# Side tasks of a planned attention kernel hand TensorE single groups of 512 columns instead of pairs, and the order is remade

## The chip, the core and the metric

The kernel runs on one core of a Trainium2 chip. The metric is the device time of one execution in microseconds. All times here are medians of several runs or come from one profiled execution, and the text says which.

## What is computed

Two attention blocks read the same input and are mixed by a gate. The reference, cut to its core (S = 2048, D = 512, 32 heads of 16 columns):

```python
g = sigmoid((x * gate_w).sum(-1, keepdims=True))
# A: softmax attention
scores = einsum("bhqd,bhkd->bhqk", q, k) * (Dh ** -0.5)
a = einsum("bhqk,bhkd->bhqd", softmax(scores), v) @ A_wo
# B: linear attention, phi(t) = where(t > 0, t + 1, exp(t)) + 1e-6
kv = einsum("bhsd,bhse->bhde", phi(k), v);  z = phi(k).sum(over s)
b = (einsum("bhqd,bhde->bhqe", phi(q), kv) / (phi(q) . z + 1e-6)) @ B_wo
out = g * a + (1 - g) * b
```

Each block has its own q, k, v (x times a 512 x 1536 matrix).

## The kernel before

**Units.** The softmax block is cut into 2048 units: one head, 512 query columns, 128 keys. Four heads stand in the four row strips of TensorE (K of 16 rows padded to 32), so a score group S is up to four matmuls of 512 columns that run beside each other (`s_fn`, built by `cand_s`). Each unit's scores fill one PSUM bank of 128 x 512. There are eight banks, and one of them gathers the attention's result.

**Two ways to the exponential.** Of each S group the first two units usually lie in two banks side by side and go to ScalarE, one activation of 128 x 1024 (line 1141, `cand_exp`, tile P). The others go to VectorE, which makes an approximate power of two from the scores in int16 (tile Z), two banks at once (line 1053) or one bank (line 1089, `cand_op1`); GpSimd adds two shifted copies of it (line 1115, `cand_shift`), whose sum with weights is the exponential. TensorE then multiplies P or Z with the values: a PV group of up to four matmuls of 17 x 512 in the four column strips (`cand_pv`, tiles Vp and Vs; the 17th row is the softmax's sum).

**Side tasks.** All else is written as generators that yield one step at a time, an operation with its engine and what it reads and writes: the projections K (`t_k`), Q (`t_q`) and V (`t_v`), phi of the linear block's keys (`t_phik`), x times phi(k) (`t_mt`), the sums and the state (`t_z`, `t_kv`, `t_m`), phi of its queries (`t_phiq`), the denominators (`t_den`), the gathering of a finished round (`aout`) and the last products with both output matrices for 128 rows (`t_final`). Their matmuls stand in the four column strips (`mm4`: 4 matmuls of 32 x 512), so one product over 128 rows of the contraction is one quad, and `pe4` packs a list of quads into one step. A step is indivisible: its matmuls stand one after the other on TensorE, and the last of them alone raises TensorE's semaphore.

**The order is made by a planner in the kernel.** It runs when the program is built. Each engine has a time at which it is free, each tile a time at which it is written or read. At each turn all candidates (a score group, a PV group, an exponential, a VectorE or GpSimd operation, the next step of the first few side tasks by due time) are compared by when they could start and by a priority, and the first is issued. The knobs of these choices stand in the dictionary `DEF`, and the table `PLAN` has a row of other values for each eight units issued (257 rows, lines 181 to 439). `TS` gives release and due times of the side tasks. Where TensorE would idle for 200 ns and more, `fill` puts dummy matmuls. TensorE has two forms here: S groups in row form, all else in column form; the planner counts a change between them.

**Waits.** Each engine has one semaphore, raised by each step (`_Eng.add`, `emit`); every matmul of the kernel but those of two transposes is recorded at line 639 (`mm`), so tiles tell them apart. DMAs are issued from SyncE's queue (lines 619 to 623): the masked copies of Q (eight of 16 KB for each of 15 tiles), the way of a finished round through DRAM (`oad`, transposed into `OAT`), the denominators, the outputs.

Of the kernel before, what the change touches and what calls it, by code (L numbers as in the profile page):

```python
# [145 lines left out]
def bass_gated_mix__mha_block__linear_attn_block__prompt_kernel(  # L146
# [22 lines left out]
    def spl(t):  # L169
# [12 lines left out]
        0: {"DSL": 0.0, "PWN": 600.0, "RIDE": 600.0, "SLK": -100.0, "REL": 1.0, "TST": 610, "PRE": 150, "O1P": 440, "ACP": 450, "EAR": 300.0, "RSV": 400.0, "TMX": 2.0, "O1W": 300.0},  # L182
        1: {"SKEW": 0, "PWT": 250.0, "HP": 160.0, "SLK": -100.0, "UEX": 0.6, "REL": 0.5, "PORT": 1, "TST": 900, "SWP": -1, "TMX": 2.0},
        2: {"DSL": 0.0, "PWT": 250.0, "HP": 160.0, "HD": 200.0, "NDB": 1, "SLK": -100.0, "UEX": -0.3, "REL": 1.0, "PORT": 1, "SGL": 410, "TST": 900, "O1P": 440, "EAR": 300.0, "RSV": 400.0, "DMX": 4.0},
        3: {"PWT": 100.0, "TPR": 650, "HD": 60.0, "NDB": 1, "UEX": -0.3, "REL": 1.0, "PORT": 1, "SGL": 410, "O1P": 410, "SWP": 1, "EAR": 300.0},
        4: {"PWT": 250.0, "HD": 0.0, "NDB": 1, "SLK": 250.0, "ROOM": 2, "REL": 1.0, "PORT": 1, "TST": 900, "O1P": 440, "EAR": 300.0, "RSV": 200.0, "DMX": 4.0},
        5: {"DSL": 0.0, "DTOL": 250.0, "PWN": 100.0, "UEX": -0.3, "REL": 1.0, "PORT": 1, "SGL": 410, "TST": 900, "PRE": 0, "O1P": 440, "EAR": 300.0, "NAJ": 1.0},
        6: {"PWN": 100.0, "NDB": 1, "REL": 1.0, "PORT": 1, "SGL": 410, "PRE": 300, "O1P": 440, "EAR": 300.0, "O1W": 300.0, "DMX": 2.0, "NAJ": 1.0},
        7: {"PWE": 100.0, "HD": 60.0, "NDB": 1, "SLK": -100.0, "PORT": 1, "SGL": 410, "PRE": 150, "O1P": 440, "SWP": 1, "EAR": 300.0, "TMX": 2.0, "NAJ": 1.0},
        8: {"SKEW": 3, "DSL": 0.0, "PWT": 100.0, "PWN": 900.0, "HP": 160.0, "HD": 0.0, "NDB": 1, "SLK": -100.0, "REL": 0.5, "SGL": 410, "TST": 900, "O1P": 440, "EAR": 150.0, "TMX": 2.0, "NAJ": 1.0},  # L190
        9: {"SKEW": 6, "PWN": 900.0, "HD": 0.0, "UEX": -0.3, "SGL": 395, "TST": 610, "ACP": 450, "SWP": 1, "NAJ": 1.0},
        10: {"PWN": 900.0, "HD": 0.0, "SLK": -100.0, "SGL": 395, "TST": 900, "PRE": 150, "O1P": 410, "SWP": 1, "TMX": 2.0, "NAJ": 1.0},
        11: {"PWN": 200.0, "TPR": 450, "SLK": -100.0, "TOP": 800, "REL": 1.0, "PRE": 0, "O1P": 440, "SWP": -1, "EAR": 300.0, "TMX": 2.0},
        12: {"DSL": 40.0, "DTOL": 2000.0, "PWE": 100.0, "PWN": 200.0, "TOP": 800, "PORT": 1, "PRE": 150, "SWP": 1, "DMX": 4.0, "NAJ": 1.0},
        13: {"SKEW": 6, "DTOL": 2000.0, "PWT": 250.0, "PWN": 100.0, "TPR": 650, "SLK": -100.0, "REL": 1.0, "SGL": 410, "TST": 900, "O1P": 440, "SWP": -1, "EAR": 900.0, "TMX": 2.0, "DMX": 4.0, "NAJ": 1.0},
        14: {"SKEW": 6, "DTOL": 2000.0, "PWT": 250.0, "PWN": 100.0, "TPR": 650, "RIDE": 900.0, "SLK": -100.0, "REL": 1.0, "SGL": 410, "TST": 900, "O1P": 440, "SWP": 1, "EAR": 900.0, "TMX": 2.0, "DMX": 4.0, "NAJ": 1.0},
        15: {"SKEW": 6, "DSL": 40.0, "PWN": 900.0, "TPR": 450, "RIDE": 900.0, "HD": 60.0, "UEX": 0.6, "ROOM": 2, "REL": 1.0, "SGL": 395, "TST": 610, "ACP": 450, "SWP": 1},
        16: {"SKEW": 0, "DSL": 150.0, "PWE": 50.0, "PWT": 250.0, "PWN": 900.0, "TPR": 720, "RIDE": 1800.0, "HP": 160.0, "HD": 60.0, "UEX": 0.6, "REL": 0.5, "TST": 900, "PRE": 0, "O1P": 440, "SWP": 1, "TMX": 2.0},
        17: {"SKEW": 6, "UEX": -0.3, "REL": 1.0, "PORT": 1, "SGL": 395, "TST": 610, "ACP": 450, "SWP": 1, "NAJ": 1.0},
        18: {"SKEW": 6, "PWT": 250.0, "PWN": 100.0, "SLK": -100.0, "REL": 1.0, "SGL": 410, "TST": 900, "O1P": 440, "SWP": -1, "EAR": 900.0, "TMX": 2.0},  # L200
        19: {"PWT": 250.0, "HP": 160.0, "HD": 60.0, "SLK": -100.0, "ROOM": 2, "REL": 1.0, "PORT": 1, "SGL": 410, "TST": 900, "PRE": 0, "O1P": 440, "SWP": 1, "TMX": 2.0, "DMX": 4.0},
        20: {"DTOL": 2000.0, "PWT": 250.0, "TPR": 720, "RIDE": 600.0, "HD": 60.0, "SLK": 0.0, "REL": 1.0, "PORT": 1, "TST": 610, "PRE": 0, "O1P": 440, "SWP": 1, "TMX": 2.0, "DMX": 2.0},
        21: {"DTOL": 2000.0, "PWT": 250.0, "TPR": 720, "RIDE": 600.0, "HD": 60.0, "SLK": 0.0, "ROOM": 2, "REL": 1.0, "PORT": 1, "TST": 610, "PRE": 0, "O1P": 440, "ACP": 450, "SWP": 1, "TMX": 2.0, "DMX": 2.0},
        22: {"DTOL": 1000.0, "PWT": 250.0, "TPR": 720, "RIDE": 600.0, "HD": 60.0, "SLK": 0.0, "ROOM": 2, "REL": 1.0, "PORT": 1, "TST": 610, "PRE": 0, "O1P": 440, "ACP": 450, "TMX": 2.0, "DMX": 2.0},
        23: {"PWE": 100.0, "PWT": 250.0, "TPR": 650, "HP": 160.0, "SLK": 0.0, "ROOM": 2, "REL": 1.0, "SGL": 410, "TST": 900, "PRE": 150, "O1P": 440, "ACP": 450, "SWP": 1, "DMX": 4.0},
        24: {"SKEW": 6, "PWT": 250.0, "PWN": 100.0, "SLK": -100.0, "REL": 1.0, "SGL": 410, "TST": 900, "O1P": 440, "SWP": -1, "EAR": 900.0, "TMX": 2.0},
        25: {"SKEW": 6, "PWN": 100.0, "SLK": -100.0, "REL": 1.0, "SGL": 410, "TST": 900, "O1P": 440, "SWP": -1, "EAR": 900.0, "TMX": 2.0},
        26: {"PWT": 250.0, "HP": 160.0, "SLK": -100.0, "ROOM": 1, "REL": 1.0, "PORT": 1, "SGL": 410, "TST": 900, "PRE": 300, "O1P": 440, "SWP": 1, "TMX": 2.0, "DMX": 4.0},
        27: {"PWT": 250.0, "HP": 160.0, "ROOM": 2, "REL": 1.0, "PORT": 1, "SGL": 410, "TST": 900, "PRE": 150, "O1P": 440, "ACP": 450, "SWP": 1, "TMX": 2.0, "DMX": 4.0},
        28: {"TPR": 450, "TOP": 800, "ROOM": 2, "REL": 1.0, "SGL": 410, "TST": 900, "PRE": 0, "O1P": 440, "SWP": -1, "EAR": 300.0, "TMX": 2.0},  # L210
        29: {"PWN": 100.0, "TPR": 450, "RIDE": 2500.0, "UEX": 1.0, "SGL": 395, "PRE": 300, "SWP": 1, "EAR": 900.0},
        30: {"PWN": 100.0, "TPR": 450, "RIDE": 2500.0, "UEX": 1.0, "SGL": 395, "PRE": 300, "SWP": 1, "EAR": 900.0},
        31: {"DTOL": 250.0, "PWN": 100.0, "ROOM": 1, "PORT": 1, "SGL": 410, "PRE": 0, "EAR": 900.0, "TMX": 2.0},
        32: {"TPR": 650, "RIDE": 900.0, "HD": 0.0, "SLK": -100.0, "PORT": 1, "O1P": 440, "EAR": 900.0, "RSV": 400.0, "TMX": 2.0, "DMX": 4.0},
        33: {"PWE": 100.0, "PWN": 600.0, "RIDE": 300.0, "HP": 220.0, "UEX": 0.6, "PORT": 1, "SGL": 395, "PRE": 0, "SWP": 1, "EAR": 900.0, "DMX": 4.0},
        34: {"SKEW": 6, "DSL": 40.0, "TPR": 450, "UEX": 0.6, "REL": 1.0, "SGL": 395, "TST": 610, "ACP": 450, "NAJ": 1.0},
        35: {"DSL": 0.0, "HP": 220.0, "HD": 0.0, "NDB": 1, "SLK": -100.0, "ROOM": 1, "REL": 1.0, "SGL": 410, "TST": 900, "PRE": 150, "O1P": 440, "SWP": 1, "RSV": 400.0, "TMX": 2.0, "DMX": 4.0, "NAJ": 1.0},
# [229 lines left out]
    with ExitStack() as es:  # L447
# [63 lines left out]
        def bank(b, n=1):  # L511
            return ps[:, 512 * b:512 * (b + n)]
# [1435 lines left out]
```

## Time and profile before

| what | value |
|---|---|
| time, median of 3 runs | 626.16 us (625.57 to 626.61) |
| the profiled execution, in all | 625.57 us |
| its span, first to last instruction | 623.8 us |
| granted TensorE clock | 1.00 |
| TensorE, VectorE, ScalarE, GpSimd busy | 99%, 96%, 98%, 76% of the span |
| instructions PE, DVE, ACT, POOL | 8432, 941, 682, 802 |

In the profile PE is TensorE, PEld its weight loads, DVE VectorE, ACT ScalarE, POOL GpSimd, SPq the queue of DMAs that SyncE issues. A row of groups reads: line, engine, operation, written tile <- read tiles, shape, count | busy us in all, mean ns of one | idle time just before, and what ended it. A row of a timeline reads: start, length, engine, line, operation, count, and in brackets idle time before it. Rows of the same kind that follow each other are merged. Ends of matmuls are modelled, so a busy TensorE needn't be at its peak; an activation overlaps with the one before it, so its length is longer than its share of the engine's time.

### The profile page before, as it was taken

The page shows a single profiled execution, that of the slowest core. Times are in us where ns is not written, and L with a number is a line of the kernel's source. Part 1 is how long each engine was busy: PE and PEld are TensorE (multiplying, and loading weights), DVE is VectorE, ACT ScalarE, POOL GpSimd, SP SyncE. Part 2 cuts the span into 40 slices and gives each one's busy share as a digit, 9 for nine tenths or more (in the row PEclk, how much of TensorE's full clock was granted, in tenths as well). Part 3 has the DMA queues.
Part 4 walks back from the last instruction along what each step waited for, and adds up shares of the span by engine and source line. Part 5 has one row for each costly group of instructions (what it writes and reads, how often), then busy time and mean ns, then how long its engine had stood idle before and what let it go on. Part 6 is the DMA issues. An engine that isn't in the chain of part 4 may idle for free.

```text
span 623.8 us, 19766 instructions
## 1 busy us (share of the span) xinstructions
PE 615.6 (99%) x8432; PEld 187.5 (30%) x8432; DVE 596.5 (96%) x941; ACT 610.2 (98%) x682; POOL 471.4 (76%) x802
## 2 busy tenths in 40 slices
PE   8999999999999999999999999999999999999998
PEld 4432322433222222322222222222222222222343
DVE  6999999999999999999999999999999999999995
ACT  6999999999999999999999999999999999999996
POOL 4576687677687889866867687767899788987893
PEclk9999999999999999999999999999999999999999
DMA  6802003001110010111101010121100101010101
GB/s 147 219 22 23 14 3 52 2 2 28 36 26 3 10 26 3 19 45 25 50 9 23 29 39 22 39 50 51 27 9 15 31 11 35 3 18 27 19 11 36
DMA packets 68367, 19.64 MB, mean 31 GB/s; under 512 B 56500, under 2 KB 68148, under 8 KB 68280
## 3 DMA queue, kind: packets, MB, share of 16 engines
q1 hardware_dynamic: 67464, 17.99, 12.9%
q8 instruction: 66, 1.08, 0.7%
q10 hardware_dynamic: 816, 0.39, 0.2%
q14 instruction: 21, 0.17, 0.1%
HBM read 8.92 MB, written 4.46 MB: 21 GB/s over the span
## 4 chain that ended last, share of the span: by engine, by line
ACT 70%; PE 28%; DMA 1%; SPq 0%; issue 0%
ACT P L1141 69%; PE ps L639 28%; ACT eb L1494 1%; DMA wA<-in_A_wqkv_dram 1%; PE ps L1343 0%; SPq L623 0%; ACT P L1642 0%; ACT KT L1319 0%
## 5 line engine op out<-in xcount | busy, mean ns | idle before, releaser
L1141 ACT ACTIVATE P<-ps 128x1024 bf16<-128x1024 f32 x642 | 597.2, 1131 | 3.0 <-PE ps L639 2.9
L1115 POOL INT64_ADD Z<-Z x784 | 466.2, 612 | 141.3 <-DVE Z L1089 103.1
L1089 DVE TENSOR_SCALAR Z<-ps 128x512 int16<-128x512 f32 x534 | 348.2, 680 | 10.9 <-PE ps L639 8.8
L639 PE MATMUL ps<-Qz,KT 32*128 32x512 bf16 x2048 | 254.9, 384 | 3.2 <-ACT P L1141 1.6
L639 PE MATMUL ps<-Z,Vs 128*17 128x512 bf16 (+1 forms) x1620 | 250.2, 370 | 0.1
L639 PE MATMUL ps<-P,Vp 128*17 128x512 bf16 (+1 forms) x1366 | 237.3, 369 | 0.0
L639 PE MATMUL ps<-Z,Vp 128*17 128x512 bf16 (+1 forms) x810 | 188.5, 370 | 0.0
L1053 DVE TENSOR_SCALAR Z<-ps 128x1024 int16<-128x1024 f32 x115 | 139.8, 1216 | 3.4 <-PE ps L639 1.3
L639 PEld LDWEIGHTS ps<-Qz,KT 32*128 32x128 bf16 x2048 | 66.1, 91 | 249.2 <-ACT P L1141 216.7
L639 PEld LDWEIGHTS ps<-Z,Vs 128*17 128x17 bf16 x1620 | 59.1, 89 | 47.8 <-issue 29.5
L639 PEld LDWEIGHTS ps<-P,Vp 128*17 128x17 bf16 x1366 | 56.2, 89 | 54.5 <-issue 36.5
L639 PEld LDWEIGHTS ps<-Z,Vp 128*17 128x17 bf16 x810 | 44.8, 88 | 20.2 <-issue 11.6
L639 PE MATMUL ps<-xT,wA 128*32 128x512 bf16 (+2 forms) x560 | 37.0, 364 | 0.4 <-DMA wA<-in_A_wqkv_dram 0.4
L1447 DVE STREAM_TRANSPOSE T<-ps 128x512 f32<-128x512 f32 x32 | 22.6, 707 | 3.4 <-PE ps L639 3.4
L1494 ACT ACTIVATE eb<-ps 128x512 bf16<-128x512 f32 x32 | 22.1, 690 | 0.0
L1496 DVE SCALAR_TENSOR_TENSOR phiK<-ps,eb 128x512 bf16<-128x512 f32 x32 | 21.7, 680 | 0.2
L639 PE MATMUL ps<-wB,OAT 128*32 128x512 bf16 x256 | 20.4, 384 | 0.0
L639 PE MATMUL ps<-wA,xT 128*32 128x256 bf16 x512 | 20.1, 275 | 0.0
L639 PE MATMUL ps<-wB,phiK 128*32 128x512 bf16 x256 | 19.3, 382 | 0.0
L639 PE MATMUL ps<-phiK,xnat 128*32 128x512 bf16 x256 | 18.6, 383 | 0.0
L639 PE MATMUL ps<-xT,wB 128*32 128x512 bf16 x256 | 17.8, 382 | 0.0
L639 PE MATMUL ps<-wB,xT 128*32 128x512 bf16 x256 | 17.4, 381 | 0.0
(81 smaller groups left out, 192.2 us busy)
## 6 DMA issues: line engine op xcount, KB each, us to landing
xnat<-rcpd SPq DMA_DIRECT2D x16, 128.0 KB
Qz<-QT SPq DMA_DIRECT2D x120, 16.0 KB, 1.8
oad<-T SPq DMA_DIRECT2D x60, 32.0 KB, 1.9
out_dram<-outt SPq DMA_DIRECT2D x14, 128.0 KB, 1.7
wB<-in_B_wqkv_dram SPq DMA_DIRECT2D x3, 512.0 KB, 6.5
wA<-in_A_wqkv_dram SPq DMA_DIRECT2D x11, 128.0 KB, 3.0
xnat<-in_A_x_dram SPq DMA_DIRECT2D x2, 512.0 KB, 8.2
xnat<-in_A_x_dram SPq DMA_DIRECT2D x6, 128.0 KB, 2.8
```

What stands on the lines that cost most here:

```text
L639: return lambda: nc.tensor.matmul(o, lhsT=l, rhs=r, start=start, stop=stop, skip_group_check=True)
L1053: res.append(C(DV, 400, 1131, lambda: nc.vector.tensor_scalar(Z[:, zs[0], :], bank(b2[0], 2), ZB, 0.0, op0=ALU.add, op1=ALU.max), [r_bank[ ...
L1089: res.append(C(DV, prio, 598, lambda: nc.vector.tensor_scalar(Z[:, z, 512 * h:512 * (h + 1)], bank(b), ZB, 0.0, op0=ALU.add, op1=ALU.max), ...
L1115: return C(PO, 300, 160 + 0.4165 * (hi - lo), lambda: nc.gpsimd.int64_add(Z[:, zw, lo:hi].bitcast(I64), Z[:, z0, lo:hi].bitcast(I64), cst) ...
L1141: return C(AC, 500, 426.5 * n + 51, lambda: nc.scalar.activation(P[:, slot:slot + n, :].rearrange("p a b -> p (a b)"), bank(bs[0], n), ACT ...
L1447: yield dv(623, lambda: nc.vector.transpose(T1[:, par, :], bank(b)), [r_bank[b]], [r_T1[par]])
L1494: yield ac(477, lambda: nc.scalar.activation(e16, bank(b), ACT.Exp), [r_bank[b]], [r_eb[i]])
L1496: yield dv(598, lambda: nc.vector.scalar_tensor_tensor(dst_ap, bank(b), 1.0 + 1e-6, e16, op0=ALU.add, op1=ALU.max), [r_bank[b], r_eb[i]], ...
```

## The change

In six of the side tasks each quad becomes a step of its own; before, two quads were one step. The steps' number of matmuls, their operands, and what VectorE and ScalarE do with the result stay. Two of the six also name fewer tiles as read, those of their own quad. `PLAN` is replaced as a whole (no row is equal); `DEF` and `TS` stay. So the order on every engine is made anew, and with it how many units go to ScalarE and to VectorE.

```diff
     PLAN = {
-        0: {"DSL": 0.0, "PWN": 600.0, "RIDE": 600.0, "SLK": -100.0, "REL": 1.0, "TST": 610, "PRE": 150, "O1P": 440, "ACP": 450, "EAR": 300.0, "RSV": 400.0, "TMX": 2.0, "O1W": 300.0},
...
+        208: {"SKEW": 6, "UEX": -0.3, "REL": 0.5, "SGL": 395, "TST": 610, "ACP": 450, "SWP": 1, "NAJ": 1.0},
...
         def t_k(t8, t, fixed=None):
...
-            for h in range(2):
-                yield pe4(512, gs[2 * h:2 * h + 2], [*r_xT[4 * t:4 * t + 4], r_wA[t8 % 2][1]], [r_bank[b]])
+            for h in range(4):
+                yield pe4(512, gs[h:h + 1], [*r_xT[4 * t:4 * t + 4], r_wA[t8 % 2][1]], [r_bank[b]])
...
         def t_mt(cb):
...
-            for t2_ in range(8):
-                gs = [mm4(bank(b), xnat[:, tb, 128 * cb:128 * (cb + 1)], phiK[:, tb, :], tb == 0, tb == NKB - 1)
-                      for tb in (2 * t2_, 2 * t2_ + 1)]
-                yield pe4(512, gs, [r_xn[2 * t2_], r_xn[2 * t2_ + 1], r_phiK[2 * t2_], r_phiK[2 * t2_ + 1]], [r_bank[b]])
+            for tb in range(NKB):
+                yield pe4(512, [mm4(bank(b), xnat[:, tb, 128 * cb:128 * (cb + 1)], phiK[:, tb, :], tb == 0, tb == NKB - 1)],
+                          [r_xn[tb], r_phiK[tb]], [r_bank[b]])
...
-            for k0, k1 in ((0, 2), (2, 4), (4, 6), (6, 7)):
-                yield pe4(512, [f(k) for k in range(k0, k1)], sum((rd(k) for k in range(k0, k1)), []), [r_bank[b]])
+            for k in range(7):
+                yield pe4(512, [f(k)], rd(k), [r_bank[b]])
```

`t_q`, `t_phik` and `t_phiq` are changed as `t_k` is. `t_v`, whose quads have 256 columns, and the small products of the start, of `t_z`, `t_kv`, `t_m`, `t_den` and the gate stay.

More of the change, by code (lines that the diff above doesn't have):

```diff
@@ new lines, in bass_gated_mix__mha_block__linear_attn_block__prompt_kernel @@
+        41: {"DTOL": 250.0, "PWE": 50.0, "PWN": 100.0, "RIDE": 300.0, "HD": 0.0, "SLK": -100.0, "REL": 1.0, "PRE": 0, "O1P": 440, "SWP": 1, "TMX": 2.0},
+        42: {"DTOL": 250.0, "PWE": 50.0, "PWN": 100.0, "RIDE": 300.0, "HD": 0.0, "SLK": -100.0, "REL": 1.0, "PRE": 0, "O1P": 440, "SWP": 1, "TMX": 2.0},
+        43: {"DTOL": 5000.0, "PWN": 100.0, "TPR": 650, "HD": 300.0, "SLK": 0.0, "ROOM": 4, "REL": 1.0, "LD": 4, "SGL": 410, "TST": 900, "O1P": 410, "EAR": 900.0, "TMX": 2.0, "DMX": 4.0, "NAJ": 1.0},
@@ new lines, in bass_gated_mix__mha_block__linear_attn_block__prompt_kernel @@
+        75: {"SKEW": 0, "DSL": 40.0, "DTOL": 1000.0, "PWT": 400.0, "PWN": 200.0, "RIDE": 300.0, "REL": 1.0, "SGL": 395, "TST": 900, "SWP": 1, "EAR": 150.0},
+        76: {"SKEW": 2, "DSL": 40.0, "DTOL": 1000.0, "PWT": 400.0, "PWN": 200.0, "RIDE": 300.0, "REL": 1.0, "PORT": 1, "SGL": 395, "TST": 900, "SWP": 1, "EAR": 150.0},
+        77: {"SKEW": 0, "DTOL": 1000.0, "UEX": -0.3, "PORT": 1, "SGL": 395, "TST": 610, "ACP": 450, "SWP": 1, "NAJ": 1.0},
+        78: {"SKEW": 0, "DTOL": 1000.0, "UEX": -0.3, "PORT": 1, "SGL": 395, "TST": 610, "ACP": 450, "SWP": 1, "NAJ": 1.0},
@@ new lines, in bass_gated_mix__mha_block__linear_attn_block__prompt_kernel @@
+        175: {"DTOL": 1000.0, "PWN": 600.0, "RIDE": 600.0, "SLK": 0.0, "ROOM": 2, "SGL": 410, "JIT": 14, "SWP": -1, "EAR": 900.0},
+        176: {"SKEW": 6, "ROOM": 2, "REL": 1.0, "SGL": 395, "TST": 610, "ACP": 450, "SWP": 1, "NAJ": 1.0},
+        177: {"SKEW": 2, "DTOL": 1000.0, "PWN": 600.0, "RIDE": 600.0, "HD": 60.0, "SLK": 0.0, "ROOM": 2, "REL": 0.5, "SGL": 410, "SWP": -1, "EAR": 900.0},
+        178: {"SKEW": 2, "PWT": 250.0, "PWN": 900.0, "HP": 160.0, "HD": 60.0, "SLK": -100.0, "UEX": -0.3, "ROOM": 4, "REL": 1.0, "SGL": 410, "TST": 900, "PRE": 300, "O1P": 410, "TMX": 2.0, "DMX": 4.0},
@@ new lines, in bass_gated_mix__mha_block__linear_attn_block__prompt_kernel @@
+        240: {"DSL": 300.0, "PWE": 100.0, "HD": 200.0, "TST": 900, "PRE": 0, "O1P": 410, "SWP": -1, "TMX": 2.0, "DMX": 4.0},
+        241: {"DSL": 300.0, "PWE": 100.0, "HD": 200.0, "TST": 900, "PRE": 0, "JIT": 5, "O1P": 410, "SWP": -1, "TMX": 2.0, "DMX": 4.0},
+        242: {"SKEW": 6, "DSL": 300.0, "DTOL": 5000.0, "PWN": 100.0, "TPR": 650, "SLK": 0.0, "REL": 1.0, "LD": 4, "SGL": 410, "TST": 900, "O1P": 410, "EAR": 300.0, "TMX": 2.0, "DMX": 4.0, "NAJ": 1.0},
+        243: {"SKEW": 3, "DSL": 40.0, "DTOL": 1000.0, "PWT": 250.0, "RIDE": 300.0, "SLK": 120.0, "REL": 1.0, "SGL": 395, "TST": 900, "SWP": 1, "EAR": 150.0},
@@ L1383, in t_q @@
             gs = proj4(b, lambda cc: w_[:, cc, :], lambda cc: xT[:, cc, 512 * qc:512 * (qc + 1)])
-            for h in range(2):
-                yield pe4(512, gs[2 * h:2 * h + 2], [*r_xT[4 * qc:4 * qc + 4], r_wA[t8 % 2][0]], [r_bank[b]])
+            for h in range(4):
+                yield pe4(512, gs[h:h + 1], [*r_xT[4 * qc:4 * qc + 4], r_wA[t8 % 2][0]], [r_bank[b]])
             s = n % NQZ
@@ L1503, in t_phik @@
             gs = proj4(b, lambda cc: xT[:, cc, 128 * tb:128 * (tb + 1)], lambda cc: wB[:, cc, D:2 * D])
-            for h in range(2):
-                yield pe4(512, gs[2 * h:2 * h + 2], [r_xT[tb], r_wB[1]], [r_bank[b]])
+            for h in range(4):
+                yield pe4(512, gs[h:h + 1], [r_xT[tb], r_wB[1]], [r_bank[b]])
             yield from phi(b, phiK[:, tb, :], [r_phiK[tb]])
@@ L1560, in t_phiq @@
             gs = proj4(b, lambda cc: wB[:, cc, 128 * i:128 * (i + 1)], lambda cc: xT[:, cc, 512 * qc:512 * (qc + 1)])
-            for h in range(2):
-                yield pe4(512, gs[2 * h:2 * h + 2], [*r_xT[4 * qc:4 * qc + 4], r_wB[0]], [r_bank[b]])
+            for h in range(4):
+                yield pe4(512, gs[h:h + 1], [*r_xT[4 * qc:4 * qc + 4], r_wB[0]], [r_bank[b]])
             yield from phi(b, phiQT[:, 4 * qc + i, :], [r_phiK[4 * qc + i]])
```

497 lines of the change are left out of this document (241 added, 256 removed).

## The prediction

> **What bounds the kernel now.** I read the page first (busy times, chain, costliest groups), then the chain in order of time, then ScalarE's own timeline, then TensorE's.
>
> ```profile
> span 623.8 us, 19766 instructions
> ...
> PE 615.6 (99%) x8432; PEld 187.5 (30%) x8432; DVE 596.5 (96%) x941; ACT 610.2 (98%) x682; POOL 471.4 (76%) x802
> ...
> ACT 70%; PE 28%; DMA 1%; SPq 0%; issue 0%
> ...
> L1141 ACT ACTIVATE P<-ps 128x1024 bf16<-128x1024 f32 x642 | 597.2, 1131 | 3.0 <-PE ps L639 2.9
> ```
>
> The chain in order of time (start, length, what):
>
> ```profile
> 13.16 79.86 PE ps L639 x1155
> ...
> 106.45 56.58 PE ps L639 x878
> 163.05 2.86 ACT P L1141 x3
> 165.92 110.46 ACT P L1141 x120
> ...
> 411.71 188.11 ACT P L1141 x205
> 599.86 17.44 PE ps L639 x328
> ```
>
> Three engines look full, but a share of busy time doesn't say which is the limit. The chain does: up to 163.05 us it runs through TensorE, then through ScalarE's exponentials to 599.86, then through TensorE's tail. The hand-over at 163.05 means that ScalarE and TensorE are nearly even: ScalarE takes a pair of score tiles as soon as TensorE has it, and TensorE writes the next pair as soon as a bank pair is free. Who is late by a little decides each time.
>
> How much is lost to being late has to be read from ScalarE's own rows (start, length, form, count, idle before):
>
> ```profile
> 7.73 1.94 ACT L1141 ACTIVATE P<-ps 128x1024 bf16<-128x1024 f32 x2 [0.35 <-PE ps L639]
> 9.55 0.38 ACT L1307 CAST KT<-ps 128x256 bf16<-128x256 f32 x1
> 10.26 2.85 ACT L1141 ACTIVATE P<-ps 128x1024 bf16<-128x1024 f32 x3 [0.32 <-PE ps L639]
> 13.61 3.77 ACT L1141 ACTIVATE P<-ps 128x1024 bf16<-128x1024 f32 x4 [0.50 <-PE ps L639]
> 17.57 2.85 ACT L1141 ACTIVATE P<-ps 128x1024 bf16<-128x1024 f32 x3 [0.19 <-PE ps L639]
> 21.68 24.14 ACT L1141 ACTIVATE P<-ps 128x1024 bf16<-128x1024 f32 x26 [1.25 <-PE ps L639]
> 45.74 0.60 ACT L1431 ACTIVATE eb<-ps 128x512 f32<-128x512 f32 x1
> ...
> 279.00 2.02 ACT L1141 ACTIVATE P<-ps 128x1024 bf16<-128x1024 f32 x2
> 280.81 0.70 ACT L1494 ACTIVATE eb<-ps 128x512 bf16<-128x512 f32 x1
> 281.29 2.06 ACT L1141 ACTIVATE P<-ps 128x1024 bf16<-128x1024 f32 x2
> ...
> 411.36 205.93 ACT L1141 ACTIVATE P<-ps 128x1024 bf16<-128x1024 f32 x224
> ```
>
> From 279.00 to 280.81 are two exponentials back to back: 0.905 us each (a row's length holds 0.21 more, the last one's overlap with what follows). The exponential of a side task holds 0.48 (280.81 to 281.29). The 224 from 411.36 to 617.29 take 205.72 without the overlap, 0.918 each: 3.0 us more than 224 x 0.905, although the row shows no idle time. An activation that starts a little late hides in the overlap. For the whole stretch from 21.68 to 617.29: 595.40 without the overlap, less 630 x 0.905 (642, and 2 + 3 + 4 + 3 are earlier), less 33 x 0.48 (one of L1431 and 32 of L1494, by the row below) = 595.40 - 570.15 - 15.84 = **9.4 us of late starts**, in a stretch that the page calls full.
>
> ```profile
> L1494 ACT ACTIVATE eb<-ps 128x512 bf16<-128x512 f32 x32 | 22.1, 690 | 0.0
> ```
>
> Before 21.68 the gap of 1.25 us is the largest among the exponentials.
>
> Why they are late shows in TensorE's rows. A quad is four 512-column matmuls in the four column strips; S is a score group.
>
> ```profile
> 97.96 0.39 PE L639 MATMUL ps<-Qz,KT 32*128 32x512 bf16 x3
> 98.28 0.61 PE L639 MATMUL ps<-wB,xT 128*32 128x512 bf16 x8
> 98.83 0.39 PE L639 MATMUL ps<-Qz,KT 32*128 32x512 bf16 x3
> ```
>
> ```profile
> 251.58 0.39 PE L639 MATMUL ps<-Qz,KT 32*128 32x512 bf16 x3
> 251.90 1.05 PE L639 MATMUL ps<-phiK,xnat 128*32 128x512 bf16 x16
> 252.88 0.39 PE L639 MATMUL ps<-Qz,KT 32*128 32x512 bf16 x4
> ```
>
> Two quads between two S: 0.87 us from S to S. Four quads: 1.30. So a quad is 0.215, and S with its two changes between row and column form is 0.44. ScalarE needs 0.905 per S. A cycle of two quads keeps up, one of three (1.08) loses 0.18, one of four loses 0.39 unless ScalarE had a pair in hand. Four cycles in a row keep up to 8.65 quads (4 x 0.905 = 3.62, less 4 x 0.44, over 0.215).
>
> **The change, part by part.** Counts are from the order of instructions of the two kernels as built.
>
> *Same work, cut finer.* The products of K, Q, phi(k), MT, phi(q) and of the final tasks stay, in single quads instead of pairs. TensorE gets 2133 semaphore updates instead of 1937. What an update costs the trace bounds: the cycle above has two quads of one update; this one has two quads with an update each (eight PV matmuls, the first and the last shown):
>
> ```profile
> 96.01 0.40 PE L639 MATMUL ps<-Qz,KT 32*128 32x512 bf16 x4
> 96.34 0.39 PE L639 MATMUL ps<-Z,Vp 128*17 128x512 bf16 x1
> ...
> 96.57 0.38 PE L639 MATMUL ps<-Z,Vs 128*17 128x512 bf16 x1
> 96.88 0.39 PE L639 MATMUL ps<-Qz,KT 32*128 32x512 bf16 x3
> ```
>
> 96.01 to 96.88 is 0.87 again. So an update costs 0.00 us with a resolution of 0.01: between -2.0 and +2.0 us for 196, and I take 0, the row's own value. The Trainium skill ("TensorE: Matmul & The Clock Gate", The cost: per-tile semaphore tail) says the opposite: increments serialise, about 26 ns each, which would be an estimate of 5.2 us for 196. The two cycles here don't show it.
>
> *ScalarE.* 644 exponentials instead of 642, the rest equal: 2 x 0.905 = **+1.8 us**, on the engine that carries the chain from 163 us on. Nothing hides it.
>
> *VectorE* has 566 single tiles instead of 534 and 97 pairs instead of 115:
>
> ```profile
> L1089 DVE TENSOR_SCALAR Z<-ps 128x512 int16<-128x512 f32 x534 | 348.2, 680 | 10.9 <-PE ps L639 8.8
> L1053 DVE TENSOR_SCALAR Z<-ps 128x1024 int16<-128x1024 f32 x115 | 139.8, 1216 | 3.4 <-PE ps L639 1.3
> ```
>
> Busy 0.652 and 1.216 each: 566 x 0.652 + 97 x 1.216 = 487.0 against 488.0. Costed at nothing: VectorE idles 27 us (623.8 - 596.5). A late side copy could cost up to one cycle, 0.87.
>
> *The start.* Up to the eighth exponential both orders are equal. Ahead of the S of the thirteenth, before puts 51 quad lengths and 10 alternations of form (0.22 each by the 0.44 above, less S itself), after 46 and 11: -5 x 0.215 + 0.22 = **-0.86 us**. This is the 1.25 us gap at 21.68, so there is room for it; bounds 0 (the K copy on VectorE is late instead) and -1.25.
>
> *The middle.* This is what decides. Between the 13th S and the last, cycles of four or more quads fall from 54 to 32, those of three rise from 100 to 126, for 14 more alternations in all (643 runs of S instead of 629, 3.1 us of TensorE, spread over a 600 us in which it is even with ScalarE). Stretches of four cycles that hold ten quads or more, clearly over the 8.65, fall from 160 to 109, by 32%; the quads above 8.65 summed over all such stretches fall from 448 to 341, by 24%; stretches of twelve or more from 50 to 24, by 52%. Late starts should follow the overloaded stretches: 9.4 us x 32% = **-3.0 us**. Bounds: 0 (lateness has another cause) and 52%, -4.9. I take the middle measure.
>
> By TensorE's own count to the point where 486 exponentials are left (the chain's hand-over): 552 quad lengths and 149 alternations before, 548 and 156 after: -0.9 + 1.5 = +0.7 us. So TensorE's total is no gain, and spacing alone must bring it.
>
> The Trainium skill ("TensorEngine Tiling (Array Packing)", Key Properties) says that changing the tiling mode drains the engine, which speaks against 14 more changes. The trace agrees that a change costs (0.22 for the pair), and it is in the counts above.
>
> *The tail.* After the last product of the attention stand 15 quads instead of 14, where the last store waits:
>
> ```profile
> 619.28 0.45 DVE L1467 STREAM_TRANSPOSE OAT<-T 128x256 bf16<-128x256 bf16 x1
> 619.31 1.45 PE L639 MATMUL ps<-wB,OAT 128*32 128x512 bf16 x20
> ...
> 620.80 0.69 ACT L1642 ACTIVATE P<-ps,gg 128x512 bf16<-128x512 f32 x1 [3.51 <-PE ps L639]
> ```
>
> TensorE reaches the last 20 at 619.31 and VectorE's transpose ends at 619.73, almost together, so the extra quad shows: **+0.2 us** (bounds 0 and 0.4).
>
> Moved DMAs: their number on SyncE's queue is equal; the masked Q copies and the output stores change places.
>
> ```profile
> Qz<-QT SPq DMA_DIRECT2D x120, 16.0 KB, 1.8
> ```
>
> I cost them at nothing, covered by the three slots of the masked Q, loaded rounds ahead; without that cover one landing, 1.8 us, would stand ahead of a round.
>
> **Sum**: +1.8 - 0.86 - 3.0 + 0.2 = -1.85 us. The profiled execution has 623.8 us of span and 625.57 us in all; it would become 621.95 and 623.7. The median of the three runs is 626.16, 0.6 above it: **624.3**.
>
> **The rivals.**
>
> *Half the spacing.* Three-quad cycles lose 0.18 each, and there are 26 more of them; if late starts follow all cycles at the price 0.39 and 0.18, the priced sum goes from 54 x 0.39 + 100 x 0.18 = 39.1 to 35.2, by 10%, -0.9 us: sum +0.2, **626.4**. For it: many late starts of the long ScalarE row stand where no side task is. Against it: a cycle of three costs nothing when its neighbours are short.
>
> *Cut tasks end later (the slower side).* Four quads in one piece take 0.86 us; in four pieces, each behind an S, up to 4 x 0.87 = 3.5. A K or Q tile that ends less than one cycle ahead of the score that needs it then delays it. It decides from the point where a tile is due within 0.87 us of its first S, most of all in the start, where K is made just in time (the gap at 21.68). Price: the start's gain is gone and the middle's too, +1.8 + 0.2 = 2.0, **628.2**; with one cycle of 0.87 lost besides, 629.0. For it: two more exponentials are certain, the spacing is an inference.
>
> *The updates cost.* At the bound of 0.01 each, +2.0 on the forecast: **626.3**. Against it: the two equal cycles.
>
> That the change does not do what it says is excluded by the built order: the pairs are single quads.
>
> **How the numbers follow.** Chances: forecast 0.46, half the spacing 0.27, later ends 0.24, updates 0.03. A measurement of this kernel can tell about 0.2%, 1.25 us, from no change: below 624.9 is faster, above 627.4 slower. Forecast is faster (0.46), half the spacing and updates are the same (0.30), later ends slower (0.24). Range: from the 52% bound, -3.75 us, 622.4, to the slower rival with its one lost cycle, 629.0. The likeliest case's own range is 622.4 to 624.9.
>
> **What would show it.** 644 exponentials still at 0.905 back to back; the gap before the thirteenth at most 0.5 us; late starts between there and the last exponential about 6.4 us by the same working; S to S at 0.87 with two single quads (an update's cost would lengthen it); the tail from the last exponential to the last store 0.2 longer. Wrong would be: a thirteenth exponential as late as before, waits of scores for K, Q or the copies of VectorE in the list of waits, or late starts still above 9 us.

## The result, and the profile after

The changed kernel takes 626.99 us (median of 22 runs, 626.52 to 628.34), the kernel before 625.86 us beside it (22 runs, 625.35 to 626.61). The ratio is 1.0019, 95% interval 1.0013 to 1.0025: **slower by 1.13 us**, where 1.85 us less were forecast. The profiled executions differ by about as much, 625.0 us of span against 623.8. The time lies in the predicted range, on the side of the rivals.

The page of the changed kernel: span, busy times, the chain's shares, the costliest group.

```profile
span 625.0 us, 19748 instructions
...
PE 616.2 (99%) x8417; PEld 184.7 (30%) x8417; DVE 596.2 (95%) x955; ACT 611.4 (98%) x684; POOL 470.7 (75%) x806
...
ACT 85%; PE 12%; issue 1%; DMA 1%; DVE 0%; SPq 0%
...
L1141 ACT ACTIVATE P<-ps 128x1024 bf16<-128x1024 f32 x644 | 598.4, 1142 | 2.5 <-PE ps L639 2.5
```

ScalarE's share of the chain went from 70% to 85%. TensorE's overloaded stretches did leave the chain: from 51.87 us to the tail at 589.93 it runs nearly all through ScalarE, before only from 163.05 on. But ScalarE's own part became no shorter. The chain in order of time (start, length, what):

```profile
13.39 9.75 PE ps L639 x181
23.16 3.54 PE ps L639 x57
26.71 24.54 PE ps L639 x362
51.87 8.94 ACT P L1141 x10
```

ScalarE's own timeline, the rows that answer to those of before:

```profile
7.95 1.94 ACT L1141 ACTIVATE P<-ps 128x1024 bf16<-128x1024 f32 x2 [0.35 <-PE ps L639]
...
13.84 6.56 ACT L1141 ACTIVATE P<-ps 128x1024 bf16<-128x1024 f32 x7 [0.50 <-PE ps L639]
20.90 5.61 ACT L1141 ACTIVATE P<-ps 128x1024 bf16<-128x1024 f32 x6 [0.50 <-PE ps L639]
27.16 19.50 ACT L1141 ACTIVATE P<-ps 128x1024 bf16<-128x1024 f32 x21 [0.66 <-PE ps L639]
...
161.19 0.68 ACT L1494 ACTIVATE eb<-ps 128x512 bf16<-128x512 f32 x1
161.67 117.61 ACT L1141 ACTIVATE P<-ps 128x1024 bf16<-128x1024 f32 x128
...
282.81 0.68 ACT L1494 ACTIVATE eb<-ps 128x512 bf16<-128x512 f32 x1
283.29 2.04 ACT L1141 ACTIVATE P<-ps 128x1024 bf16<-128x1024 f32 x2
285.10 0.72 ACT L1494 ACTIVATE eb<-ps 128x512 bf16<-128x512 f32 x1
...
413.36 204.94 ACT L1141 ACTIVATE P<-ps 128x1024 bf16<-128x1024 f32 x223
622.04 0.69 ACT L1641 ACTIVATE P<-ps,gg 128x512 bf16<-128x512 f32 x1 [3.74 <-PE ps L639]
```

Four stretches of the span can be compared, each by rows of the two profiles:

| stretch | before | after | difference |
|---|---|---|---|
| start to the first exponential | 7.73 | 7.95 | +0.22 |
| first to 13th exponential | 21.68 - 7.73 = 13.95 | 20.90 - 7.95 = 12.95 | -1.00 |
| 13th to the end of the last | 617.29 - 21.68 = 595.61 | 618.30 - 20.90 = 597.40 | +1.79 |
| after it, to the span's end | 623.84 - 617.29 = 6.55 | 624.95 - 618.30 = 6.65 | +0.10 |

They add up to 1.11, the spans' difference (here to the hundredth, by the end of the trace's last instruction). The first row is no effect of the change: both orders are equal up to there, and the other runs below start between 7.75 and 8.54. The third row is two exponentials at the 0.917 found below, 1.83, less 0.04. By the prediction's own working the late starts are 597.40 - 0.21 - 632 x 0.905 - 33 x 0.48 = 9.39 us, before 9.41; forecast were 6.4.

**Those 9.4 us are not late starts.** The prediction read ScalarE's price from starts, 0.905 from one exponential to the next. Read the same rows by their ends. In the rows of after above, the activation at 282.81 ends at 283.49 and the two exponentials behind it at 285.33: 0.92 each, though their starts step by (285.10 - 283.29)/2 = 0.905. The lengths show where the difference stays: the side activation takes 0.68 there and 0.72 after the two. The rows that the prediction quotes from before say the same: 280.81 + 0.70 to 281.29 + 2.06 is 1.84 for two. Over long rows the ends step by 0.917: 161.67 + 117.61 = 279.28 for 128, from 161.87 on (the side activation at 161.19 lasts 0.68), 117.41/128. Over all steps of the trace behind the 13th, from the end of one exponential to the end of the next, the median is 0.917 us in both kernels, and the quickest 0.912 and 0.914; for a side activation it is 0.490.

So an activation may start 0.904 after the one ahead while it ends 0.917 after it, and the lengths of a row grow from 1.02 up to 1.33 us; when a start is a little late, the length shrinks again and the "late start" costs nothing. In the kernel before, for instance, the exponential at 84.50 starts 1.08 us after the one ahead, is 1.17 long where that one was 1.33, and ends 0.916 after it. What is lost over ScalarE's own rate, from the end of the 13th (its start and 1.02, the shortest length in the trace) to the last end:

- before: 617.29 - 22.70 - 629 x 0.917 - 33 x 0.489 = **1.7 us**
- after: 618.30 - 21.92 - 631 x 0.917 - 33 x 0.489 = **1.6 us**

There never were 9.4 us to win by spacing, only 1.7, and the net gain was 0.1.

### The profile page after: what moved, and what is told of

It is laid out like the page before. It is cut to its first block, busy times and chain, and to the rows that moved or that the text cites. A ratio compares the mean times of both kernels' runs of the same rounds, so it can differ in the third digit from the quotient of the medians.

```text
span 625.0 us, 19748 instructions
## 1 busy us (share of the span) xinstructions
PE 616.2 (99%) x8417; PEld 184.7 (30%) x8417; DVE 596.2 (95%) x955; ACT 611.4 (98%) x684; POOL 470.7 (75%) x806
## 3 DMA queue, kind: packets, MB, share of 16 engines
q8 instruction: 66, 1.08, 0.7%
## 4 chain that ended last, share of the span: by engine, by line
ACT 85%; PE 12%; issue 1%; DMA 1%; DVE 0%; SPq 0%
ACT P L1141 83%; PE ps L639 12%; ACT eb L1494 3%; DMA wA<-in_A_wqkv_dram 1%; PE ps L1343 0%; DVE Qz L1303 0%; SPq L623 0%; DVE eb L1495 0%; ACT P L1641 0%; DVE Z L1089 0%
## 5 line engine op out<-in xcount | busy, mean ns | idle before, releaser
L1089 DVE TENSOR_SCALAR Z<-ps 128x512 int16<-128x512 f32 x566 | 369.5, 681 | 11.2 <-PE ps L639 9.3
L639 PE MATMUL ps<-Qz,KT 32*128 32x512 bf16 x2048 | 258.4, 385 | 2.7 <-ACT P L1141 1.7
L639 PE MATMUL ps<-Z,Vs 128*17 128x512 bf16 (+1 forms) x1612 | 254.6, 370 | 0.0
L639 PE MATMUL ps<-Z,Vp 128*17 128x512 bf16 (+1 forms) x806 | 192.7, 370 | 0.7 <-DVE T L1447 0.6
L1053 DVE TENSOR_SCALAR Z<-ps 128x1024 int16<-128x1024 f32 x97 | 118.2, 1219 | 5.6 <-PE ps L639 3.9
L639 PE MATMUL ps<-xT,wA 128*32 128x512 bf16 (+2 forms) x560 | 39.5, 365 | 0.5 <-DMA wA<-in_A_wqkv_dram 0.5
L639 PE MATMUL ps<-wB,phiK 128*32 128x512 bf16 x256 | 20.9, 383 | 0.0
L639 PE MATMUL ps<-xT,wB 128*32 128x512 bf16 x256 | 19.7, 384 | 0.2
L639 PE MATMUL ps<-wB,xT 128*32 128x512 bf16 x256 | 18.9, 383 | 0.0
```

The lines of the kernel that those rows point to most:

```text
L639: return lambda: nc.tensor.matmul(o, lhsT=l, rhs=r, start=start, stop=stop, skip_group_check=True)
L1053: res.append(C(DV, 400, 1131, lambda: nc.vector.tensor_scalar(Z[:, zs[0], :], bank(b2[0], 2), ZB, 0.0, op0=ALU.add, op1=ALU.max), [r_bank[ ...
L1089: res.append(C(DV, prio, 598, lambda: nc.vector.tensor_scalar(Z[:, z, 512 * h:512 * (h + 1)], bank(b), ZB, 0.0, op0=ALU.add, op1=ALU.max), ...
```

## The experiments

What stood in question after the result: are exponentials late because of the side tasks' quads (**Side theory**), because of TensorE's whole load (**Load theory**), because of the round trip from a freed bank pair to the next exponential (**Loop theory**), or because VectorE and GpSimd hold each other up at a few places (**Collision theory**)? And is it really the number of exponentials that moves the end?

**Shorter side quads in the kernel before (e1) and in the changed one (e3).**

```diff
+        def mm4h(o, l, r, start=True, stop=True):
+            return mm4(o, l, r, True, stop) if start else mm4(o[:, 0:256], l, r[:, 0:256], False, stop)
...
-            return [mm4(bank(b), lfn(cc), rfn(cc), cc == 0, cc == nk - 1) for cc in range(nk)]
+            return [mm4h(bank(b), lfn(cc), rfn(cc), cc == 0, cc == nk - 1) for cc in range(nk)]
```

> The kernel before in its own order, but every side quad after the first of its product works on 256 of the 512 columns (the other half of those columns is left out of K, Q, phi, MT and the last products). About 358 quads lose 0.107 us each, 38 us of TensorE in all, and a run of four side quads falls from 0.86 to about 0.54 us. Late starts of ScalarE (thirteenth exponential to the end of the last, less 0.905 and 0.48 each) are 9.4 us in the kernel before. Side theory (late starts come from side steps that hold TensorE): they fall to 4 to 5 us, time 621 to 622. Load theory (late starts follow TensorE's whole load, whoever's it is): to 4 to 7 us. Loop theory (late starts come from the banks that the exponential two back has to release, whatever TensorE does): still 9 us, time within 1 us of before.

> The same half-length side quads in the changed kernel, in its own order. Side theory: the single quads have already taken what there was to take, so late starts fall less than in the kernel before, by 2 us or less. Load theory: they fall as much as there, by 3 to 5 us, and the changed kernel stays about 1.8 us (two exponentials) less the 1.0 us of its earlier start behind. Loop theory: 9 us stay.

**Shorter PV matmuls in the kernel before (e2) and in the changed one (e4).**

```diff
-                    fns.append(mm(o, v_ap(t8, pc["w"], pc["kb"], 2 * j + par), pc["ap"], start=first[q][j], stop=False))
+                    c = 512 if first[q][j] else 256
+                    fns.append(mm(o[:, 0:c], v_ap(t8, pc["w"], pc["kb"], 2 * j + par), pc["ap"][:, 0:c], start=first[q][j], stop=False))
```

> The kernel before in its own order, but the PV matmuls after the first of each head and round work on 256 of the 512 columns (the other half is left out of the sums over keys). About 840 quads lose 0.107 us, 90 us of TensorE; the side quads keep their length. Side theory: of 9.4 us of late starts the part behind runs without side quads goes, about 5.5 us stay, time about 622. Load theory: nearly all goes, 1 to 3 us stay, time 617 to 620. Loop theory: still 9 us.

> The same half-length PV matmuls in the changed kernel. Side theory: with single quads nothing but PV can be what is late, so nearly all of 9.4 us goes. Load theory: the same. Loop theory: 9 us stay. Between this and the kernel before with short PV: side theory has the changed one faster by 3 us or more, load theory slower by about 0.8 us (1.8 of two exponentials less 1.0 at the start).

All four leave out half of the columns of these products. TensorE's busy time falls by 19 us in e1 and e3 and by 49 to 51 us in e2 and e4, about half of the 38 and 90 us that were expected.

| kernel | time | ratio to before | TensorE busy | lost over 0.917 per exponential |
|---|---|---|---|---|
| before, beside e1 to e4 | 625.92 | | 615.6 | 1.6 |
| e1, before with short side quads | 624.28 | 0.9974 (0.9964 to 0.9983) | 596.3 | 0.4 |
| e2, before with short PV | 627.02 | 1.0025 (1.0011 to 1.0039) | 566.4 | 3.1 |
| after, beside 625.86 | 626.99 | 1.0019 (1.0013 to 1.0025) | 616.2 | 1.5 |
| e3, after with short side quads | 626.38 | 1.0008 (0.9999 to 1.0018) | 597.2 | 1.6 |
| e4, after with short PV | 627.16 | 1.0027 (1.0016 to 1.0039) | 565.4 | 1.9 |

The last column is the sum of all steps from one exponential's end to the next less 0.917, over some 630 steps of the trace; those that end with a side activation are left out, so it is up to 0.1 below the sums above. About 1.5 of e2's 3.1 us are lost around two stretches in which its trace shows TensorE's granted clock at 0.50 to 0.70 (from 302 to 306 and from 452 to 460 us), so half of this loss stands beside a slower TensorE; e4's execution shows 1.00 throughout. The page of e4:

```profile
PE 565.4 (90%) x8417; PEld 188.7 (30%) x8417; DVE 596.7 (95%) x955; ACT 611.6 (98%) x684; POOL 470.5 (75%) x806
```

TensorE has 51 us less to do, ScalarE is as busy as before, and the time doesn't fall. Load theory is out for the kernels as they are. Side theory holds for one part, and falls far short of its 621 to 622: in the kernel before, the side quads cause 1.1 of the 1.6 us (e1), and by no more than that could spacing help. In the changed kernel they cause none (e3), yet as much is lost there, at other places (below). Loop theory seems to come true: by the working of the expectations, with 0.905 and 0.48, 8.3, 11.0, 9.4 and 9.7 us stay in e1 to e4. But some 7.6 of them are only the difference between 0.917 and 0.905, and whether the banks or ScalarE itself make that difference is shown by the next two runs.

**Ten exponentials made twice, early (e5) and late (e6), in the kernel before.** The first of the two results goes to a spare tile that nobody reads.

```diff
+        TWICE = range(20, 150, 13)
...
-            return C(AC, 500, 426.5 * n + 51, lambda: nc.scalar.activation(
...
+            f2 = lambda: nc.scalar.activation(spare[:, 0:512 * n], bank(bs[0], n), ACT.Exp, scale=ESC)
+            return C(AC, 500, 426.5 * n + 51, [f2, f] if nexp[0] in TWICE else f,
```

In e6 the range is `range(430, 600, 17)`.

> The kernel before in its own order; ten exponentials between the 20th and the 150th are made twice (the first time into a tile that nobody reads). That is the stretch where the chain runs through TensorE. If every exponential is on the path: +9.0 us, 0.905 each. If the late starts of that stretch (2.9 us) take some up because TensorE is the one that leads there: +6 to +7 us.

> The same with ten exponentials between the 430th and the 600th, where the chain runs through ScalarE. On the path: +9.0 us. If the late starts of the stretch (3.0 us in 224) are slack that the next exponential can take up: +6 to +8 us. Either way two exponentials more, as in the changed kernel, cost between 1.2 and 1.8 us.

e5 takes 635.19 us, ratio 1.0146 (1.0131 to 1.0162), and e6 635.05 us, 1.0146 (1.0133 to 1.016), beside 625.91: 9.3 and 9.1 us for ten, **0.92 each**, wherever they stand, also in the first 163 us, where the chain of before ran through TensorE. So each added exponential is on the path in full. These times can't tell 0.917 from 0.905, which for ten differ by 0.1 us while the intervals are 1.7 to 1.9 us wide; the rows can. One of the doubles in ScalarE's timeline of e5:

```profile
35.77 6.67 ACT L1146 ACTIVATE P<-ps 128x1024 bf16<-128x1024 f32 x7
42.31 1.04 ACT L1148 ACTIVATE spare<-ps 128x1024 bf16<-128x1024 f32 x1
43.21 4.79 ACT L1146 ACTIVATE P<-ps 128x1024 bf16<-128x1024 f32 x5
```

The row of seven ends at 42.44, the spare one at 43.35, 0.91 later, and nothing behind it gives the time back. The second of the two reads the same banks again and waits for no score group, and by the trace it still ends 0.916 after the first, although it starts 0.90 after it (42.31 to 43.21). In all twenty doubles of e5 and e6 this step is 0.914 to 0.919. So the 0.917 is ScalarE's own, not the round trip through the banks, and Loop theory is out as its cause.

**Collisions of VectorE and GpSimd (e7, e8).** Three exponentials of the changed kernel end 0.1 to 0.3 us late (at 34.60, 92.41 and 93.59; 0.11, 0.12 and 0.27 over 0.917) behind a VectorE operation that took longer than its like. VectorE in the changed kernel, then GpSimd beside it:

```profile
31.24 0.58 DVE L1424 COPY gwr<-gwc 128x128 bf16<-128x128 bf16 x1
...
90.59 0.73 DVE L1495 TENSOR_SCALAR eb<-eb 128x512 bf16<-128x512 bf16 x1
```

```profile
90.56 1.23 POOL L1115 INT64_ADD Z<-Z  x2 [0.28 <-DVE Z L1089]
```

e7 makes the copy at 31.24 with strided operands; e8 is e7 with a tiny memset on GpSimd ahead of the addition at 90.56, so that the addition comes behind VectorE's start.

```diff
-nc.vector.tensor_copy(gwr[:], gwc[:].unsqueeze(2).to_broadcast([128, NCC, 32]))
+nc.vector.tensor_copy(gwr[:].rearrange("p c k -> p k c"), gwc[:].unsqueeze(1).to_broadcast([128, 32, NCC]))
...
+            g = lambda: nc.gpsimd.memset(dummy[:, 2:3], 0.0)
+            return C(PO, 300, 160 + 0.4165 * (hi - lo), [g, f] if (batch["u"], w) == ([(3, 13, 2), (3, 14, 1)], 1) else f,
```

> The changed kernel in its own order; VectorE's copy of the gate's weights (0.58 us beside a running GpSimd add, 0.26 in the kernel before) writes with a stride and the same result. Collision theory (two VectorE operations that a GpSimd add holds up make three exponentials late by 0.65 us in all): the copy takes under 0.3 us and the exponential at 34.60 us is no longer late, -0.2 us. Without the theory: no change.

> As e7, and ahead of the GpSimd add that starts 0.03 us before VectorE's phi operation at 90.59 us stands a small memset on GpSimd, so that the add comes after VectorE's start. Collision theory: the phi operation takes 0.3 instead of 0.73 us, the exponentials at 92.41 and 93.59 come 0.45 us earlier, -0.65 us in all, time 626.3. Without it: no change, or +0.1 from the memset.

e7 takes 627.18 us, 1.0019 (1.001 to 1.0027): nothing won. Its copy became longer, not shorter, so that half of Collision theory is not tested by it:

```profile
31.46 0.81 DVE L1424 COPY gwr<-gwc 128x128 bf16<-128x128 bf16 x1
```

e8 takes 626.54 us, 1.0013 (1.0004 to 1.0022), 0.64 less than e7. The profiled executions differ by 0.9: 0.43 is a first exponential that came earlier (7.75 against 8.18), 0.4 is the collision, since what is lost over 0.917 falls from 1.6 to 1.2. VectorE and GpSimd in e8:

```profile
90.52 0.29 DVE L1497 TENSOR_SCALAR eb<-eb 128x512 bf16<-128x512 bf16 x1
```

```profile
90.47 0.10 POOL L1117 MEMSET dummy<- 128x1 f32 x1 [0.25 <-DVE Z L1089]
90.54 2.94 POOL L1115 INT64_ADD Z<-Z  x6
```

So this collision is real and worth 0.4 us in the profiled execution. It does not explain the 1.13.

**Four exponentials cut short (e9), and the same with short PV (e10).**

```diff
+        SHORT = (250, 350, 450, 550)
...
+            c = 32 if nexp[0] in SHORT else 512 * n
...
-                P[:, slot:slot + n, :].rearrange("p a b -> p (a b)"), bank(bs[0], n), ACT.Exp, scale=ESC),
+                P[:, slot:slot + n, :].rearrange("p a b -> p (a b)")[:, 0:c], bank(bs[0], n)[:, 0:c], ACT.Exp, scale=ESC),
```

> The changed kernel with four of its 644 exponentials (the 250th, 350th, 450th and 550th) made on 32 columns instead of 1024; the rest of those eight score tiles is left out, everything else is issued as before. By the end-to-end steps of 0.917 us for 1024 columns and 0.489 for 512, a column costs 0.84 ns and the short ones about 0.09 each, so 0.83 is saved by each. Rate theory (ScalarE's own step of 0.917 carries the whole middle, TensorE has time in hand): 4 x 0.83 = 3.3 us less than the changed kernel's 626.99, 623.7, and below the kernel before because the start is 0.8 earlier. Balance theory (TensorE is as late as ScalarE, so ScalarE can't run ahead of it): no gain, 627.0, with a gap in front of each exponential that follows a short one.

> The same four short exponentials in the changed kernel whose PV matmuls after the first of each sum stream 256 of 512 columns (half of those products are left out). That kernel alone took 627.16. Rate theory: 627.16 - 3.3 = 623.9, the same gain as without the shorter PV matmuls. Balance theory: 623.9 too, but here alone, with 627.0 where TensorE has all its work.

e9 takes 626.31 us, 1.0005 (0.9996 to 1.0014), and e10 626.58, 1.0017 (1.0006 to 1.0027). That is 0.7 and 0.6 less than without the cut, 0.17 and 0.15 for each, where Rate theory gave 0.83. Both theories fell as they were put: the gain is not 3.3 in either kernel, and TensorE's load makes no difference. The gap that Balance theory forecast is there, but for another reason. e9 around the first short one, the second of the first row (ScalarE, TensorE's loads and matmuls, ScalarE again):

```profile
247.58 1.33 ACT L1146 ACTIVATE P<-ps 128x1024 bf16<-128x1024 f32 x2
...
248.87 0.09 PEld L639 LDWEIGHTS ps<-Qz,KT 32*128 32x128 bf16 x2 [0.27 <-ACT P L1146]
248.87 0.39 PE L639 MATMUL ps<-Qz,KT 32*128 32x512 bf16 x2
...
249.30 3.90 ACT L1146 ACTIVATE P<-ps 128x1024 bf16<-128x1024 f32 x4 [0.40 <-PE ps L639]
```

The short one is done at 248.91, but the next exponential starts at 249.30: its S was waiting for the bank pair of the exponential two back and could begin only at 248.87, and from S to exponential is 0.43. With two bank pairs, two steps can't be quicker than 0.05 (from the exponential's end to S) + 0.43 + 1.02 = 1.50 us, against 2 x 0.917 = 1.83; this is an estimate from these rows. By it one exponential that vanishes can give back 0.33 at most, and in e10, where TensorE has time, VectorE takes part of that (VectorE, TensorE and ScalarE in e10, behind the third short one):

```profile
440.57 1.27 DVE L1089 TENSOR_SCALAR Z<-ps 128x512 int16<-128x512 f32 x2
...
441.30 0.09 PEld L639 LDWEIGHTS ps<-Qz,KT 32*128 32x128 bf16 x1 [0.46 <-DVE Z L1089]
...
441.72 1.94 ACT L1146 ACTIVATE P<-ps 128x1024 bf16<-128x1024 f32 x2 [0.17 <-PE ps L639]
```

The S has a part for VectorE too, and its last matmul waits for VectorE's operation on the bank; the exponential is 0.17 late.

**The cut without an order made for it (e11).** The changed generators with the table of before; the edit is shown against the changed kernel.

```diff
     PLAN = {
-        0: {"DSL": 0.0, "DTOL": 2000.0, "PWN": 600.0, "SLK": 250.0, "REL": 1.0, "TST": 610, "PRE": 150, "O1P": 440, "ACP": 450, "EAR": 300.0, "RSV": 400.0, "TMX": 2.0, "O1W": 300.0},
+        0: {"DSL": 0.0, "PWN": 600.0, "RIDE": 600.0, "SLK": -100.0, "REL": 1.0, "TST": 610, "PRE": 150, "O1P": 440, "ACP": 450, "EAR": 300.0, "RSV": 400.0, "TMX": 2.0, "O1W": 300.0},
...
```

> Single side quads of the changed kernel, with the table of planning numbers of the kernel before: the cut without the order remade for it. Its order as built has 683 exponentials where the kernel before has 642 (78 of them filled with one score tile by the planner). Rate theory: 41 exponentials more, 41 x 0.917 = 37.6 us, and some us of gaps: about 664 to 672. If the cut by itself evened out TensorE's work, exponentials would be late for fewer us in all than the 9.4 of both kernels; Rate theory expects no less than 9.4.

One execution takes 673.71 us, 2 us above the expected 664 to 672. ScalarE makes 683 exponentials, and 11.8 us are lost over 0.917, not less than in the two kernels:

```profile
L1141 ACT ACTIVATE P<-ps 128x1024 bf16<-128x1024 f32 x683 | 635.9, 1123 | 12.2 <-PE ps L639 11.6
```

41 exponentials more at 0.917 are 37.6 of its 47.9 us, and the additional loss 10.2 of them. With a table that was not made for it the cut evens out nothing; the order decides, and first of all by how many pairs it gives to ScalarE.

**Every exponential a little shorter (e12), and with short PV (e13).** A step removed at one place strains one hand-over; this spreads it.

```diff
+            c = 512 * n - 16 if nexp[0] >= 30 else 512 * n
...
-                P[:, slot:slot + n, :].rearrange("p a b -> p (a b)"), bank(bs[0], n), ACT.Exp, scale=ESC),
+                P[:, slot:slot + n, :].rearrange("p a b -> p (a b)")[:, 0:c], bank(bs[0], n)[:, 0:c], ACT.Exp, scale=ESC),
```

> The changed kernel with every exponential from the 31st on made on 1008 of its 1024 columns (the last 16 are left out): 614 x 16 x 0.84 ns = 8.2 us less work on ScalarE alone, spread evenly, so that no single hand-over is strained as by the four short exponentials. Rate theory: ScalarE's step sets the middle, 626.99 - 8.2 = 618.8. Level theory (ScalarE, TensorE and VectorE take the score groups from each other and are level to a per cent, so that lightening one only moves the wait to the next): a gain of 1 to 3 us, 624 to 626, the steps from end to end spread above 0.904 with waits for S, and a late total far above the 1.5 us that both kernels show over 0.917.

> The same in the changed kernel whose PV matmuls after the first of each sum stream 256 of 512 columns (half of those products left out; 627.16 without the 1008). Rate theory: 619.0. Level theory with TensorE as the next limit: clearly below the run with TensorE's whole work, since TensorE has 90 us less here. Level theory with VectorE as the next limit: the same gain as there, 1 to 3 us, and waits of S for VectorE's copies.

e12 takes 623.19 us, 0.996 (0.9945 to 0.9975), and e13 620.6 us, 0.9923 (0.9906 to 0.9939). Of 8.2 us on ScalarE 3.8 come through with TensorE's whole work and 6.6 (from 627.16) with 51 us less of it. ScalarE's last long stretch in e12, then in e13:

```profile
412.01 202.63 ACT L1145 ACTIVATE P<-ps 128x1008 bf16<-128x1008 f32 x222
```

```profile
412.09 199.53 ACT L1145 ACTIVATE P<-ps 128x1008 bf16<-128x1008 f32 x220
```

By starts and without the overlap of 0.2, 0.912 and 0.906 each; the median step from end to end is 0.903 in both. So ScalarE's rate is the limit at 0.917, and when it is lightened by 14 ns TensorE stops it a little short of half way, at 0.912. TensorE is the next limit by less than one per cent, and VectorE isn't: in e13, with VectorE's work as it was, four fifths of the gain come through. Rate theory (618.8) was too simple, and Level theory's 624 to 626 too pessimistic by 0.8.

## Why the prediction was wrong, step by step

- **ScalarE, +1.8: right.** Two exponentials cost 0.92 each when they are added (e5, e6), 1.83 us. VectorE took four score tiles fewer (566 + 2 x 97 = 760 instead of 534 + 2 x 115 = 764), and these are the two pairs.
- **The start, -0.86: right up to the 13th exponential**, -1.00 from the first to it, but most of it is lost again soon. The gap at 21.68 fell from 1.25 to 0.50. Part of a bound named there did come up six exponentials later, where a copy of K on VectorE is late instead (the wait list of the changed kernel between 25.5 and 27.2 us, and the copy, which ends 0.06 us before S starts at 26.71):

```profile
PEld ps L639 <- DVE KT L1372: 0.3, 1, 0.3
```

```profile
25.97 0.68 DVE L1372 CAST KT<-ps 128x512 bf16<-128x512 f32 x1
26.71 0.12 PEld L639 LDWEIGHTS ps<-Qz,KT 32*128 32x128 bf16 x6 [0.29 <-DVE KT L1372]
```

  It makes the gap of 0.66 us at 27.16, and that exponential ends 0.76 us late, so only a quarter of the 1.00 is left at the 19th. The 0.76 is the one large part of the middle's 1.6 us. A late tile is the mechanism of the slower rival, at one place only; that the cut of the K task made it late is not shown, since VectorE was busy with other work right up to the copy.
- **The middle, -3.0: wrong, and this is the step that failed.** The counts were right: cycles of four quads and more did become fewer, and TensorE did leave the chain between 51.87 and 163.05. The 9.4 us that they were to save a third of were wrong. They came from 630 x 0.905, a price taken from two starts in a row; 630 x (0.917 - 0.905) = 7.6 us of them are ScalarE's own work, as the doubles of e5 and e6 show. The prediction saw the 0.918 of the 224 last exponentials and read it as being late, with "the row shows no idle time" beside it. A third of the 1.7 us that were really lost would have been -0.5; the runs give -0.1. The steps of the trace show why: in the kernel before the late ends are scattered, 0.35 at 163.05 and the others 0.14 or less; in the changed one 0.76 stand at 27.16, 0.39 behind the collision at 90.59 and 0.11 behind the gate's copy, and under 0.4 is left. With e1 and e3 this fits that spacing took what the side quads cost, about 1.1, and that the new order lost as much at these three places. With +1.8, -0.9, -0.5 and +0.2 the sum would have been +0.6 instead of -1.85.
- **The tail, +0.2: right.** From the last exponential's end to the last activation's start 3.51 became 3.74; 0.10 of it reaches the span's end.
- **Updates at nothing: right.** Two single side quads with an update each stand between two S in the changed kernel (TensorE):

```profile
88.47 0.39 PE L639 MATMUL ps<-Qz,KT 32*128 32x512 bf16 x3
88.79 0.61 PE L639 MATMUL ps<-wB,xT 128*32 128x512 bf16 x8
89.34 0.39 PE L639 MATMUL ps<-Qz,KT 32*128 32x512 bf16 x3
```

  0.87 from S to S, as with one update before. The 26 ns per increment of the Trainium skill ("TensorE: Matmul & The Clock Gate", The cost: per-tile semaphore tail) don't show at this spacing.
- **The rivals.** "Half the spacing" came near in time (626.4) by luck, for a reason that the runs don't bear out: at the 10% of its own count the 9.4 us would have been 8.5. A tile that came late, as "Cut tasks end later" has it, happened once, for 0.76 us.

Open remains whether an order with single quads and 642 exponentials exists that keeps the start's 1.0 us. e9 shows that pairs can't simply be left away: with the S groups as they are, a vanished exponential gives 0.15 to 0.17 back, and not its whole step.

## What to carry to other kernels

Take an engine's price per instruction from the ends of a long row that shows no idle time, not from the starts of a short one: an overlap that grows makes the starts look quicker than the engine is, and over 630 instructions 12 ns become 7.6 us of waits that don't exist. Before a gain is put on better spacing, work out what the limiting engine loses over that price; that is the ceiling. And in an order that a planner makes anew, count first what the limiting engine gets more or less of.

## What the runs showed of the hardware

- Exponentials of 128 x 1024 back to back start every 0.904 us and end every 0.917; the lengths of a row grow from 1.02 up to 1.33 us, until a later start shortens one again at no cost to its end. The second of two on the same banks ends 0.914 to 0.919 after the first (e5, e6).
- From 512 to 1024 columns the step grows by 0.917 - 0.490 = 0.427 us, 0.834 ns per column; 1008 columns step by 0.903, 14 ns less for 16. The Trainium skill ("ScalarE: Activation LUTs", What ACT_TABLE_LOAD costs) says 0.833 ns per element; the trace agrees.
- A VectorE operation on SBUF that normally takes 0.29 us took 0.73 when GpSimd's addition had started 0.03 us earlier, and 0.29 when the addition started 0.02 us later, behind a memset of 0.10 us (e8). The Trainium skill ("SBUF — State Buffer", SBUF: two separate sides) calls the pair of ports that both use an exclusive lock held for a whole instruction. These rows agree that the order of the two starts decides; VectorE's operation ended 0.15 us after the first addition, which took 0.61, and so less than its own 0.29.
- Half as much streaming in the PV matmuls saved no time, and e2's profiled execution shows a mean granted clock of 0.992 where all others show 0.999 or 1.000: in two-us windows it was 0.55 and 0.60 from 302 to 306 us, and 0.59, 0.50, 0.50 and 0.70 from 452 to 460. Why is open.
